# A first MoE pass over 768 tokens in six PSUM banks, later passes of 512, and attention's copies shared out anew

## The chip, the cores and the metric

One Trainium2 chip, of which the kernel uses one core. The metric is the device time of one execution in microseconds. The engines are named as the profile names them: PE (matmuls) with PEld (its weight loads), DVE (VectorE), ACT (ScalarE), POOL (GpSimd) and SP, whose queue issues every DMA here. PSUM, which the matmuls write, has eight banks; one holds 512 float32 per partition.

## The reference

Windowed attention, then two MoE layers that act as plain two-layer networks over 2304 tokens:

```python
scores = q @ k.T / 8 - slope[h] * |i - j|      # batch 4, 8 heads, 576 positions, head size 64
attn = softmax(where(0 <= i - j < 128, scores, -1e9)) @ v
x = attn as [2304 tokens, 512]
h = x @ w1_in;  x = (h * cos(h)) @ w1_out      # w_in 512 x 2048, w_out 2048 x 512
h = x @ w2_in;  g = h if h >= 1 else 0 if h <= -1 else (h + 1)**2 / 4
out = g @ w2_out
```

## The kernel before

**Attention.** 36 pairs, each of 256 tokens and two heads. A pair goes through `do_s` (scores on PE into banks y0 to y3; DVE's fused add-and-minimum, L219; ACT's exp, L226), `normalise` (an add of 1e-9, L232, and a reciprocal, L233, on DVE; the scaling on POOL, L236), `do_t` (transposes into h0 and h1, copied to SBUF by DVE three times in four and by ACT once, `PT`) and `do_v` (banks h2 and h3, copied into `xall` by ACT, `XE`). These stages of successive pairs are interleaved.

**Weights.** They arrive as 64-bit floats in 64 halves, 32 for each layer. `to_f32` turns a half into float32: one ACT pass (L129) into a tile `wu`, of which there are three, then three DVE passes (L130, L132, L134). For layer 1 (`make_w1`) ACT rounds it to a high part (L154) and POOL subtracts for the low part (L78). For layer 2 (`keep_w2`) the float32 half is written to DRAM (`wd`, L165), and is read back and split while layer 1's last chunk runs (`split_w2`).

**MoE.** Tokens go in six chunks of 384 through layer 1, then six through layer 2. A chunk has 16 feature blocks f. `mm_a` makes h of one block with 12 matmuls (4 pieces of the model width, 3 products of high and low parts each) into one of four banks h0 to h3, in turn. `chain` makes g from it: ACT, DVE, ACT, DVE (L320, L321, L325, L326), then a high part by ACT (L337) and a low part by DVE (L78). `mm_b` adds the block into y0 to y3 with 12 more matmuls, three blocks later (`LAG`). `evict` copies y out.

**Order.** PE runs in the order in which the code is written. The other engines run in an order that a scheduler fixed when the program was built; each of them takes its instructions strictly in turn, so one that waits holds all behind it. The scheduler places `to_f32` well ahead of where the code asks for it.

Of the kernel before, what the change touches and what calls it, by code (L numbers as in the profile page):

```python
# [9 lines left out]
F32 = mybir.dt.float32  # L10
# [24 lines left out]
W2LO = "PP"  # L35
GLO = ("D", "D")
# [4 lines left out]
def attention_moe_moe_kernel(  # L41
# [18 lines left out]
    wd = dram.tile([NF, 128, 1024], F32, name="wd")  # L60
    ident = one.tile([128, 128], F32, name="ident")

    xall = one.tile([128, KD, NTOK], F32, name="xall")

    uid = [0]

    def nm(s):
# [90 lines left out]
    w2_kept = [0]  # L158
# [26 lines left out]
    dist8 = []  # L185

    def load(n):
        if n < len(pairs) and "ld" not in pairs[n]:
# [73 lines left out]
    def do_v(p):  # L262
        v_no[0] += 1
        b = ps.tile([128, 512], F32, tag=f"h{2 + v_no[0] % 2}", name=nm("pa"))
        for j in range(2):
            nb = p["w"][j] // 128
            for i in range(nb):
                for h in range(2):
# [5 lines left out]
        x = xall[:, p["hp"], p["b0"] * 128:p["b0"] * 128 + 256]  # L274
        if XE[v_no[0] % len(XE)] == "A":
            ACT.copy(x, b[:, 0:256])
        else:
# [4 lines left out]
    half_pi = one.tile([128, 1], F32, name="half_pi")  # L282

    def split_x(c):
        c["xs"] = [tuple(one.tile([128, T], F32R, tag=f"x{s}{d}", name=nm(f"x{s}")) for s in "hl")
                   for d in range(KD)]
        for d in range(KD):
            hi, lo = c["xs"][d]
            x = xall[:, d, c["t0"]:c["t0"] + T]
            ACT.copy(hi, x)  # L290
            sub_lo(DVE, lo, x, hi)

    h_no = [0]

    def mm_a(c, f):
        hi, lo = weights[c["m"], f]
        h_no[0] = (h_no[0] + 1) % 4
        h = ps.tile([128, 512], F32, tag=f"h{h_no[0]}", name=nm("h"))[:, 0:T]
        n = 0
        for d in range(KD):  # L300
            xh, xl = c["xs"][d]
            s = slice(d * 128, d * 128 + 128)
            for w, x in ((hi, xh), (hi, xl), (lo, xh)):
                PE.matmul(h, lhsT=w[:, 0, s], rhs=x, start=(n == 0), stop=(n == 11))  # L304
                n += 1
                if n == 6:
                    gap()
        chain(c, f, h)
        gap()

    def chain(c, f, h):
        t = small("t")[:, 0:T]
        gh, gl = (small(s, F32R)[:, 0:T] for s in ("gh", "gl"))
        c["g", f] = gh, gl
        if c["m"] == 0:
            k = two.tile([128, T], I32, tag="k", name=nm("k"), bufs=2)

            def s0():

# [22 lines left out]
        later(2, s1)  # L342
        later(3, s2)

    def mm_b(c, f):
# [3 lines left out]
        gh, gl = c["g", f]  # L349
        n = 0  # L350
        for d in range(KD):
            s = slice(d * 128, d * 128 + 128)
            for i, (w, x) in enumerate(((hi, gh), (hi, gl), (lo, gh))):
                PE.matmul(c["y"][d], lhsT=w[:, 1, s], rhs=x,  # L354
                          start=(f == 0 and i == 0), stop=(f == NF - 1 and i == 2))
                n += 1
                if n == 6:
                    gap()
        if f == NF - 1:
            evict(c)  # L360
        if c["m"] == 0 and c["last"]:
            split_w2(f)
        gap()

    def evict(c):
        t0 = c["t0"]
        for d in range(KD):
            s = xall[:, d, t0:t0 + T] if c["m"] == 0 else small("ys")[:, 0:T]
            if d % 2:
                ACT.copy(s, c["y"][d])  # L370
            else:
                DVE.tensor_copy(s, c["y"][d])
            if c["m"]:
                SP.dma_start(out[d * 128:(d + 1) * 128, t0:t0 + T], s)

    chunks = [dict(m=m, t0=i * T, last=i == NCH - 1) for m in range(2) for i in range(NCH)]

    def body():
        load(0)
        dist_sb = two.tile([128, 256], F32, tag="k", name="dist_sb", bufs=2)  # L380
        SP.dma_start(dist_sb, dist)
        load(1)
        DVE.memset(half, 0.5)
        DVE.memset(half_pi, TWO_PI / 4)
        for h in range(NH):

            d8 = one.tile([128, 256], F32, tag=f"x{'hl'[h % 2]}{h // 2}", name=nm("dist8"))
            POOL.tensor_scalar_mul(d8, dist_sb, 2.0 ** (3 - (h + 1)))
            dist8.append(d8)
        make_identity(nc, ident)  # L390
        np_ = len(pairs)
        steps = np_ + AHEAD + 1
        for k in range(-AHEAD, np_ + 1):
            load(k + AHEAD + 1)
            load(k + AHEAD + 2)
            if k + AHEAD < np_:
# [7 lines left out]
            while w1_done[0] * steps < (k + AHEAD) * 2 * PRE:  # L404
                make_w1()
        carried = None
        split_x(chunks[0])
        step = 0
        for ci, c in enumerate(chunks):
            nxt = chunks[ci + 1] if ci + 1 < len(chunks) else None  # L410
            for f in range(NF):
                if c["m"] == 0:
                    if ci == 0:
                        while w1_done[0] < min(2 * (f + W_AHEAD), 2 * NF):
                            make_w1()
# [12 lines left out]
                if f >= LAG:
                    mm_b(c, f - LAG)
            for f in range(NF - LAG, NF - 1):  # L430
                mm_b(c, f)
            carried = c, NF - 1
        mm_b(*carried)
# [58 lines left out]
```

## Time and profile before

| | us |
|---|---|
| runs shown, median of 3 (lowest to highest) | 980.55 (978.40 to 981.01) |
| profiled execution, its own time | 980.5 |
| its span, first to last instruction | 978.7 |
| attention, up to PE's first MoE matmul | 157.6 |
| first two chunks of layer 1, until PE no longer waits | 152.4 |
| the rest, to the last matmul | 665.2 |

Read the stretches apart: a share of the whole span says little here, since attention, the first chunks and the rest have different limits. In a row of a timeline the first number is the start and the second the length; engines overlap the end of one instruction with the start of the next, so the distance of two starts is what an instruction occupies.

### The profile page before, as it was taken

The page shows a single profiled execution, that of the slowest core. Times are in us where ns is not written, and L with a number is a line of the kernel's source. Part 1 is how long each engine was busy: PE and PEld are TensorE (multiplying, and loading weights), DVE is VectorE, ACT ScalarE, POOL GpSimd, SP SyncE. Part 2 cuts the span into 40 slices and gives each one's busy share as a digit, 9 for nine tenths or more (in the row PEclk, how much of TensorE's full clock was granted, in tenths as well). Part 3 has the DMA queues.
Part 4 walks back from the last instruction along what each step waited for, and adds up shares of the span by engine and source line. Part 5 has one row for each costly group of instructions (what it writes and reads, how often), then busy time and mean ns, then how long its engine had stood idle before and what let it go on. Part 6 is the DMA issues. An engine that isn't in the chain of part 4 may idle for free.

```text
span 978.7 us, 14930 instructions
## 1 busy us (share of the span) xinstructions
PE 936.0 (96%) x5712; PEld 894.6 (91%) x5712; DVE 583.7 (60%) x1288; ACT 456.8 (47%) x1024; POOL 176.3 (18%) x150
## 2 busy tenths in 40 slices
PE   5988888998999999999999999999999999999998
PEld 3666667987998999999999999999999999999998
DVE  6899999999898544444345463443444443534433
ACT  5677877655555444344346662332232322323322
POOL 6567665340000000000005660000000000000000
PEclk9998999998999999999999999999999999999999
DMA  6639113447787000000002320000000000000000
GB/s 246 275 121 395 46 45 108 130 151 240 253 283 255 23 2 1 1 1 1 1 1 86 123 71 1 1 33 1 1 33 1 33 1 1 33 1 1 33 1 33
DMA packets 24983, 75.02 MB, mean 77 GB/s; under 512 B 2768, under 2 KB 5968, under 8 KB 24912
## 3 DMA queue, kind: packets, MB, share of 16 engines
q1 hardware_dynamic: 24912, 74.07, 21.9%
q8 instruction: 45, 0.74, 0.3%
q14 instruction: 26, 0.21, 0.1%
HBM read 60.95 MB, written 13.11 MB: 76 GB/s over the span
## 4 chain that ended last, share of the span: by engine, by line
PE 73%; DVE 13%; DMA 5%; issue 4%; ACT 2%; POOL 2%; SPq 0%; POOLq 0%; ACTq 0%; DVEq 0%
PE y L354 35%; PE h L304 34%; DMA wst<-in_w 5%; DVE wu L132 3%; DVE wu L134 3%; DVE sc L219 1%; PE pa L205 1%; PE pa L250 1%; DVE wu L130 1%; POOL sc L236 1%; PE pa L271 1%; DVE pt L256 1%; ACT wu L129 1%; DVE gl L78 1%; ACT sc L226 1%
## 5 line engine op out<-in xcount | busy, mean ns | idle before, releaser
L354 PE MATMUL y<-gl,wh 128*128 128x384 f32 x768 | 259.4, 338 | 4.8 <-DVE gl L78 4.6
L354 PE MATMUL y<-gh,wh 128*128 128x384 f32 x768 | 258.9, 337 | 4.9 <-ACT gh L337 4.9
L354 PE MATMUL y<-gh,wl 128*128 128x384 f32 x768 | 258.2, 336 | 0.0
L304 PE MATMUL h<-xh,wh 128*128 128x384 f32 x768 | 256.8, 334 | 0.0
L304 PE MATMUL h<-xl,wh 128*128 128x384 f32 x768 | 256.7, 334 | 0.0
L304 PE MATMUL h<-xh,wl 128*128 128x384 f32 x768 | 256.6, 334 | 0.0
L78 DVE TENSOR_TENSOR gl<-t,gh 128x384 fp32r<-128x384 f32 x192 | 113.5, 591 | 91.8 <-ACT gh L337 91.5
L331 ACT ACTIVATE t<-t,half 128x384 f32<-128x384 f32 x96 | 59.2, 617 | 206.9 <-DVE t L329 206.9
L354 PEld LDWEIGHTS y<-gl,wh 128*128 128x128 f32 x768 | 145.3, 189 | 7.5 <-DVE gl L78 7.5
L354 PEld LDWEIGHTS y<-gh,wh 128*128 128x128 f32 x768 | 145.1, 189 | 7.4 <-ACT gh L337 7.4
L354 PEld LDWEIGHTS y<-gh,wl 128*128 128x128 f32 x768 | 145.5, 189 | 0.0
L304 PEld LDWEIGHTS h<-xh,wh 128*128 128x128 f32 x768 | 144.5, 188 | 0.2 <-issue 0.2
L337 ACT CAST gh<-t 128x384 fp32r<-128x384 f32 x192 | 98.4, 513 | 98.6 <-DVE t L334 59.8
L304 PEld LDWEIGHTS h<-xh,wl 128*128 128x128 f32 x768 | 144.3, 188 | 0.0
L304 PEld LDWEIGHTS h<-xl,wh 128*128 128x128 f32 x768 | 144.3, 188 | 0.0
L329 DVE TENSOR_SCALAR t<-h 128x384 f32<-128x384 f32 x96 | 53.5, 557 | 112.1 <-PE h L304 112.1
L78 POOL TENSOR_TENSOR wl<-wst,wh 128x512 fp32r<-128x512 f32 x32 | 45.0, 1430 | 315.2 <-ACT wh L175 311.3
L321 DVE SCALAR_TENSOR_TENSOR t<-h,k 128x384 f32<-128x384 f32 x96 | 53.1, 553 | 64.0 <-ACT k L320 64.0
L334 DVE TENSOR_TENSOR t<-h,t 128x384 f32<-128x384 f32 x96 | 53.5, 557 | 55.0 <-ACT t L331 55.0
L226 ACT ACTIVATE sc<-sc,st 128x256 f32<-128x256 f32 (+1 forms) x144 | 69.8, 486 | 32.6 <-DVE st L219 32.3
L236 POOL TENSOR_TENSOR sc<-sc,st 128x512 f32<-128x512 f32 (+1 forms) x72 | 77.7, 1100 | 38.6 <-ACT sc L226 12.7
L325 ACT ACTIVATE t<-t,half_pi 128x384 f32<-128x384 f32 x96 | 59.1, 616 | 45.2 <-DVE t L321 44.9
(42 smaller groups left out, 851.3 us busy)
## 6 DMA issues: line engine op xcount, KB each, us to landing
wst<-in_w SPq DMA_DIRECT2D x64, 512.0 KB, 3.8
qkv<-in_qkv SPq DMA_DIRECT2D x36, 512.0 KB, 9.1
wd<-wu SPq DMA_DIRECT2D x32, 256.0 KB, 2.6
wst<-wd SPq DMA_DIRECT2D x16, 512.0 KB, 3.3
out_t<-ys SPq DMA_DIRECT2D x24, 192.0 KB, 1.9
dist_sb<-in_dist SPq DMA_DIRECT2D x1, 128.0 KB, 3.3
```

Source lines behind the costliest of these rows:

```text
L78: eng.tensor_tensor(out=out, in0=full, in1=f32(hi), op=ALU.subtract)
L132: DVE.scalar_tensor_tensor(out=ui, in0=high, scalar=0x80000000, in1=ui, op0=ALU.bitwise_and, op1=ALU.bitwise_or)
L226: ACT.activation(sc[:, h, 0:w], sc[:, h, 0:w], AF.Exp, bias=st[:, c:c + 1], scale=-1.0, accum_out=st[:, 4 + c:5 + c])
L236: POOL.tensor_tensor(out=sc[:, :, 0:w], in0=sc[:, :, 0:w], in1=st[:, 8 + 2 * j:10 + 2 * j].unsqueeze(2).to_broadcast([128, 2, w]), op=ALU. ...
L304: PE.matmul(h, lhsT=w[:, 0, s], rhs=x, start=(n == 0), stop=(n == 11))
L321: DVE.scalar_tensor_tensor(out=t, in0=h, scalar=INV_2PI, in1=k, op0=ALU.mult, op1=ALU.subtract)
L325: ACT.activation(t, t, AF.Sin, bias=half_pi, scale=TWO_PI)
L329: DVE.tensor_scalar(out=t, in0=h, scalar1=-1.0, scalar2=1.0, op0=ALU.max, op1=ALU.min)
L331: ACT.activation(t, t, AF.Square, bias=half, scale=0.5)
L334: DVE.tensor_tensor(out=t, in0=h, in1=t, op=ALU.max)
L337: ACT.copy(gh, t)
L354: PE.matmul(c["y"][d], lhsT=w[:, 1, s], rhs=x, start=(f == 0 and i == 0), stop=(f == NF - 1 and i == 2))
```

## The change

- Layer 1's first chunk has 768 tokens, as a part of 512 and a part of 256; the other chunks have 512, and layer 2 ends with one of 256. In the first chunk h of the two parts is in h0 and h1, one bank each; y of the first part in y0 to y3, y of the second part in h2 and h3, two pieces to a bank. `mm_b` follows `mm_a` by one block there and by two blocks elsewhere.
- `xall` and the fixed xh and xl tiles give way to a pool of x tiles; `split_x` of the first chunk is written inside the attention loop. `wu` has two tiles instead of three.
- In attention DVE and ACT take the copies after the transposes in turn, and the copies of x in turn. The add of 1e-9 moves from DVE to POOL, the scaling of the distance table from POOL to DVE. `PRE` goes from 6 to 5, and `keep_w2` is spread over 42 of the 48 blocks of the later chunks.

```diff
-T = 384
-NCH = NTOK // T
-LAG = 3
+PARTS = ((((0, 512), (512, 256)), ((768, 512),), ((1280, 512),), ((1792, 512),)),
+         (((0, 512),), ((768, 512),), ((1280, 512),), ((1792, 512),), ((512, 256),)))
+KEEP_STEPS = 42
-PRE = 6
+PRE = 5
-PT = "DDDA"
-XE = "A"
+PT = "DA"
+XE = "DA"
+    chunks = [dict(m=m, parts=parts, last=i == len(PARTS[m]) - 1, lag=1 if len(parts) > 1 else 2)
-        u = two.tile([128, 512], F32, tag="wu", name=nm("wu"), bufs=3)
+        u = two.tile([128, 512], F32, tag="wu", name=nm("wu"), bufs=2)
-        DVE.tensor_scalar_add(st[:, 4:8], st[:, 4:8], 1e-9)
+        POOL.tensor_scalar_add(st[:, 4:8], st[:, 4:8], 1e-9)
-            POOL.tensor_scalar_mul(d8, dist_sb, 2.0 ** (3 - (h + 1)))
+                DVE.tensor_scalar_mul(dist8[h], dist_sb[0], 2.0 ** (3 - (h + 1)))
...
-    def mm_a(c, f):
+    def mm_a(c, i, f):
+        if len(c["parts"]) > 1:
+            tag = f"h{i}"
+        else:
+            h_no[0] = (h_no[0] + 1) % 4
+            tag = f"h{h_no[0]}"
+        w = c["parts"][i][1]
...
-            c["y"] = [ps.tile([128, 512], F32, tag=f"y{d}", name=nm("y"))[:, 0:T] for d in range(KD)]
+            if i:
+                b = [ps.tile([128, 512], F32, tag=f"h{2 + d}", name=nm("y")) for d in range(2)]
+                c["y", i] = [b[d // 2][:, d % 2 * w:d % 2 * w + w] for d in range(KD)]
...
-                mm_a(c, f)
+                for i in ps_:
+                    mm_a(c, i, f)
...
-                if f >= LAG:
-                    mm_b(c, f - LAG)
+                if f >= lag:
+                    for i in ps_:
+                        mm_b(c, i, f - lag)
```

The scheduler's order on DVE in the first MoE chunk, before, about halfway: from the first use of one block's h to that of the next. The `wu` rows are the conversion of weight halves, the rows on t, h and gl the chain.

```order
L321 SCALAR_TENSOR_TENSOR t_2473<-h_2460,k_2476 128x384
L132 SCALAR_TENSOR_TENSOR wu_2563<-wst_2552,wu_2563 128x512
L134 SCALAR_TENSOR_TENSOR wu_2563<-wst_2552,wu_2563 128x512
L326 TENSOR_TENSOR t_2473<-h_2460,t_2473 128x384
L130 TENSOR_SCALAR wu_2609<-wu_2609 128x512
L132 SCALAR_TENSOR_TENSOR wu_2609<-wst_2561,wu_2609 128x512
L78 TENSOR_TENSOR gl_2475<-t_2473,gh_2474 128x384
L321 SCALAR_TENSOR_TENSOR t_2528<-h_2515,k_2531 128x384
```

The same place in the program now, a block of the 768-token chunk (L364 and L369 are the chain's two uses of h, L80 its low part):

```order
L364 SCALAR_TENSOR_TENSOR t_2595<-h_2582,k_2598 128x512
L132 TENSOR_SCALAR wu_3654<-wu_3654 128x512
L134 SCALAR_TENSOR_TENSOR wu_3654<-wst_3609,wu_3654 128x512
L369 TENSOR_TENSOR t_2595<-h_2582,t_2595 128x512
L364 SCALAR_TENSOR_TENSOR t_2616<-h_2601,k_2618 128x256
L136 SCALAR_TENSOR_TENSOR wu_3654<-wst_3609,wu_3654 128x512
L132 TENSOR_SCALAR wu_3732<-wu_3732 128x512
L80 TENSOR_TENSOR gl_2597<-t_2595,gh_2596 128x512
L369 TENSOR_TENSOR t_2616<-h_2601,t_2616 128x256
L134 SCALAR_TENSOR_TENSOR wu_3732<-wst_3652,wu_3732 128x512
L80 TENSOR_TENSOR g_2617<-t_2616,g_2617 128x256
L136 SCALAR_TENSOR_TENSOR wu_3732<-wst_3652,wu_3732 128x512
```

A block now carries two chains and, with the rest of its rows, three converted halves, where it carried one chain and about one and a half halves. In both programs 17 halves stand ahead of the first chain; ahead of the last chain of the first 768 tokens stand 60 before and 59 now.

POOL in the middle of attention, before: two scalings (sc) for each pair, and the low part of a weight half now and then.

```order
L78 TENSOR_TENSOR wl_1489<-wu_1492,wh_1488 128x512
L236 TENSOR_TENSOR sc_1089<-sc_1089,st_1080 128x512
L236 TENSOR_TENSOR sc_1094<-sc_1094,st_1080 128x512
L236 TENSOR_TENSOR sc_1145<-sc_1145,st_1136 128x512
L236 TENSOR_TENSOR sc_1150<-sc_1150,st_1136 128x512
```

POOL now, between two pairs:

```order
L80 TENSOR_TENSOR wl_927<-wu_930,wh_926 128x512
L256 TENSOR_SCALAR st_728<-st_728 128x4
L260 TENSOR_TENSOR sc_737<-sc_737,st_728 128x512
L260 TENSOR_TENSOR sc_742<-sc_742,st_728 128x512
L80 TENSOR_TENSOR wl_927<-wu_1127,wh_926 128x512
```

The small add (L256) now stands in POOL's queue behind the scalings and the low part that come before it, and DVE's reciprocal, on which the next scaling waits, follows it.

## Rows read from the trace of the kernel before

**Rows 1.** Page, part 1: busy us of each engine (share of the span) x instructions.
```profile
PE 936.0 (96%) x5712; PEld 894.6 (91%) x5712; DVE 583.7 (60%) x1288; ACT 456.8 (47%) x1024; POOL 176.3 (18%) x150
```

**Rows 2.** Windows: stretch, its length, PE, PEld, DVE, ACT, POOL busy, clock, DMA.
```profile
0.00:157.60 157.60, 128.15 (x1104) 92.33 (x1104) 138.00 (x498) 112.14 (x377) 103.81 (x100) 0.96 0.47 179
157.60:310.00 152.40, 142.69 (x774) 137.46 (x773) 143.15 (x248) 90.74 (x172) 27.50 (x18) 0.97 0.65 210
310.00:975.20 665.20, 665.15 (x3838) 664.83 (x3836) 302.57 (x544) 253.45 (x475) 44.98 (x32) 1.00 0.06 21
975.20:978.70 3.50, 0.00 (x0) 0.00 (x0) 0.03 (x1) 0.47 (x1) 0.00 (x0) 0.90 0.59 210
```

**Rows 3.** The chain of waits: start, length, what; at full clock and early on.
```profile
168.57 3.51 PE y L354 x11
...
346.99 2.08 PE y L354 x12
```

**Rows 4.** Windows of PE alone around 169 us: busy, granted clock.
```profile
157.60:164.00 6.40, 6.40 (x38) 1.00 0.55 175
164.00:174.00 10.00, 8.13 (x36) 0.83 0.31 99
```

**Rows 5.** Groups by form, 50 to 150 us: busy, mean ns | idle before, releaser.
```profile
L236 POOL TENSOR_TENSOR sc<-sc,st 128x512 f32<-128x512 f32 x49 | 54.4, 1130 | 34.1 <-ACT sc L226 12.7 <-PE pa L205 9.8 <-DVE st L233 4.2
...
L219 DVE CUSTOM_DVE_ANT_0 sc<-pa,dist 128x256 f32<-128x256 f32 x96 | 35.8, 413 | 1.6 <-PE pa L205 1.4
...
L256 DVE COPY pt<-pa 128x512 f32<-128x512 f32 x36 | 23.7, 672 | 0.5 <-PE pa L250 0.4
...
L232 DVE TENSOR_SCALAR st<-st 128x4 f32<-128x4 f32 x26 | 11.5, 443 | 1.6 <-ACT sc L226 1.5
```

**Rows 6.** Tile st, the same stretch: ns min/median/max.
```profile
L232 DVE TENSOR_SCALAR st<-st x26: 151/364/1031, 51.5 to 147.8; 128x4 f32<-128x4 f32 x26
```

**Rows 7.** Groups by form, whole run: smaller tables, copies and POOL's smallest instruction.
```profile
L388 POOL TENSOR_SCALAR dist<-dist_sb 128x256 f32<-128x256 f32 x8 | 6.7, 848 | 3.5 <-DMA dist_sb<-in_dist 3.3
...
L256 DVE COPY pt<-pa 128x256 f32<-128x256 f32 x6 | 2.5, 415 | 1.6 <-PE pa L250 1.6
...
L482 POOL MEMSET const-float32-0.0<- 128x1 f32 x1 | 0.1, 98 | 0.2 <-issue 0.2
```

**Rows 8.** Timeline, first MoE chunk: a conversion step on DVE beside POOL.
```profile
175.56 1.76 POOL L78 TENSOR_TENSOR wl<-wu,wh 128x512 fp32r<-128x512 f32 x1 [7.46 <-ACT wh L154]
...
176.09 1.52 DVE L130 TENSOR_SCALAR wu<-wu 128x512 uint32<-128x512 uint32 x1
177.53 0.55 DVE L326 TENSOR_TENSOR t<-h,t 128x384 f32<-128x384 f32 x1
```

**Rows 9.** Timeline of DVE later, without POOL: one half's three steps and a chain step.
```profile
264.06 0.43 DVE L130 TENSOR_SCALAR wu<-wu 128x512 uint32<-128x512 uint32 x1 [0.67 <-ACT wu L129]
264.52 0.69 DVE L132 SCALAR_TENSOR_TENSOR wu<-wst,wu 128x512 uint32<-128x512 uint32 x1
265.13 0.55 DVE L321 SCALAR_TENSOR_TENSOR t<-h,k 128x384 f32<-128x384 f32 x1
265.60 0.68 DVE L134 SCALAR_TENSOR_TENSOR wu<-wst,wu 128x512 uint32<-128x512 uint32 x1
```

**Rows 10.** Windows of line L134, once for each half converted: layer 1, then layer 2.
```profile
175.20:221.20 46.00, 11.65 (x14) 1.00 0.47 146
222.60:310.00 87.40, 19.05 (x28) 0.96 0.79 259
```

**Rows 11.** Tile wu, whole run: ns min/median/max; the store's landing in us.
```profile
L129 ACT ACTIVATE wu<-wst x64: 644/671/709, 10.6 to 311.8; 128x512 f32<-128x512 f32 x64
...
DMA to landing us min/median/max: 2.0/2.6/3.9
```

More of the change, by code (lines that the diff above doesn't have):

```diff
@@ L61, in attention_moe_moe_kernel @@
     ident = one.tile([128, 128], F32, name="ident")
-    xall = one.tile([128, KD, NTOK], F32, name="xall")
+    chunks = [dict(m=m, parts=parts, last=i == len(PARTS[m]) - 1, lag=1 if len(parts) > 1 else 2)
+              for m in range(2) for i, parts in enumerate(PARTS[m])]
+    all_parts = [p for parts in PARTS[0] for p in parts]
     uid = [0]
@@ L184, in attention_moe_moe_kernel, with new_x, free_x, x_lo @@
     pairs = [dict(b0=b0, hp=hp) for b0 in range(0, NBLK, 2) for hp in range(NH // 2)]
-    dist8 = []
+    x_tiles = {}
+    x_free = {512: list(range(17)), 256: list(range(4))}
+    def new_x(w, dtype=F32):
+        size = w if x_free[w] else 512
+        slot = size, x_free[size].pop(0)
+        return one.tile([128, size], dtype, tag=f"x{size}.{slot[1]}", name=nm("x"))[:, 0:w], slot
+    def free_x(slot):
+        x_free[slot[0]].append(slot[1])
+    dist8 = {}
+    dist_sb = []
+    def x_lo(n):
+        return one.tile([128, 512 if n < 4 else 256], F32R, tag=f"xl{n}", name=nm("xl"))
     def load(n):
@@ L198, in do_s @@
         banks = []
+        for h in (2 * hp, 2 * hp + 1):
+            if h not in dist8:
+                dist8[h] = x_lo(h)[:, 0:256].bitcast(F32)
+                DVE.tensor_scalar_mul(dist8[h], dist_sb[0], 2.0 ** (3 - (h + 1)))
         for j in range(2):
@@ L273, in do_v @@
                               start=(i == 0), stop=(i == nb - 1))
-        x = xall[:, p["hp"], p["b0"] * 128:p["b0"] * 128 + 256]
+        t0 = p["b0"] * 128
+        o, w = max(a for a in all_parts if a[0] <= t0)
+        if (o, p["hp"]) not in x_tiles:
+            x_tiles[o, p["hp"]] = new_x(w)
+        x = x_tiles[o, p["hp"]][0][:, t0 - o:t0 - o + 256]
         if XE[v_no[0] % len(XE)] == "A":
@@ L284, in split_x @@
     def split_x(c):
[L285 to L291, printed above, removed]
+        c["xs"] = []
+        for i, (o, w) in enumerate(c["parts"]):
+            xs = []
+            for d in range(KD):
+                x, slot = x_tiles.pop((o, d))
+                hi, hi_slot = new_x(w, F32R)
+                lo = x_lo(4 * i + d)[:, 0:w]
+                ACT.copy(hi, x)
+                sub_lo(DVE, lo, x, hi)
+                free_x(slot)
+                xs.append((hi, lo, hi_slot))
+            c["xs"].append(xs)
     h_no = [0]
-    def mm_a(c, f):
+    def mm_a(c, i, f):
         hi, lo = weights[c["m"], f]
-        h_no[0] = (h_no[0] + 1) % 4
-        h = ps.tile([128, 512], F32, tag=f"h{h_no[0]}", name=nm("h"))[:, 0:T]
+        if len(c["parts"]) > 1:
[4 more added lines that the diff above has]
+        w = c["parts"][i][1]
+        h = ps.tile([128, 512], F32, tag=tag, name=nm("h"))[:, 0:w]
         n = 0
         for d in range(KD):
-            xh, xl = c["xs"][d]
+            xh, xl, _ = c["xs"][i][d]
             s = slice(d * 128, d * 128 + 128)
-            for w, x in ((hi, xh), (hi, xl), (lo, xh)):
-                PE.matmul(h, lhsT=w[:, 0, s], rhs=x, start=(n == 0), stop=(n == 11))
+            for a, x in ((hi, xh), (hi, xl), (lo, xh)):
+                PE.matmul(h, lhsT=a[:, 0, s], rhs=x, start=(n == 0), stop=(n == 11))
                 n += 1
@@ L307, in mm_a, with chain @@
                     gap()
-        chain(c, f, h)
+        chain(c, i, f, h)
         gap()
[L311 to L314, printed above, removed]
+    def chain(c, i, f, h):
+        w = c["parts"][i][1]
+        t = small("t")[:, 0:w]
+        if i:
+            g = small("g", F32R)
+            gh, gl = g[:, 0:w], g[:, w:2 * w]
+        else:
+            gh, gl = (small(s, F32R)[:, 0:w] for s in ("gh", "gl"))
+        c["g", i, f] = gh, gl
         if c["m"] == 0:
-            k = two.tile([128, T], I32, tag="k", name=nm("k"), bufs=2)
+            k = two.tile([128, 512], I32, tag="k", name=nm("k"), bufs=2)[:, 0:w]
             def s0():
@@ L343, in chain, with mm_b @@
         later(3, s2)
-    def mm_b(c, f):
+    def mm_b(c, i, f):
         if f == 0:
-            c["y"] = [ps.tile([128, 512], F32, tag=f"y{d}", name=nm("y"))[:, 0:T] for d in range(KD)]
+            w = c["parts"][i][1]
+            if i:
+                b = [ps.tile([128, 512], F32, tag=f"h{2 + d}", name=nm("y")) for d in range(2)]
+                c["y", i] = [b[d // 2][:, d % 2 * w:d % 2 * w + w] for d in range(KD)]
+            else:
+                c["y", i] = [ps.tile([128, 512], F32, tag=f"y{d}", name=nm("y"))[:, 0:w]
+                             for d in range(KD)]
         hi, lo = weights[c["m"], f]
-        gh, gl = c["g", f]
+        gh, gl = c["g", i, f]
         n = 0
@@ L352, in mm_b @@
             s = slice(d * 128, d * 128 + 128)
-            for i, (w, x) in enumerate(((hi, gh), (hi, gl), (lo, gh))):
-                PE.matmul(c["y"][d], lhsT=w[:, 1, s], rhs=x,
-                          start=(f == 0 and i == 0), stop=(f == NF - 1 and i == 2))
+            for k, (a, x) in enumerate(((hi, gh), (hi, gl), (lo, gh))):
+                PE.matmul(c["y", i][d], lhsT=a[:, 1, s], rhs=x,
+                          start=(f == 0 and k == 0 and not (i and d % 2)),
+                          stop=(f == NF - 1 and k == 2 and (i == 0 or d % 2 == 1)))
                 n += 1
@@ L363, in mm_b, with evict @@
         gap()
-    def evict(c):
-        t0 = c["t0"]
+    def evict(c, i):
+        o, w = c["parts"][i]
         for d in range(KD):
-            s = xall[:, d, t0:t0 + T] if c["m"] == 0 else small("ys")[:, 0:T]
+            if c["m"] == 0:
+                x_tiles[o, d] = new_x(w)
+                s = x_tiles[o, d][0]
+            else:
+                s = small("ys")[:, 0:w]
             if d % 2:
-                ACT.copy(s, c["y"][d])
+                ACT.copy(s, c["y", i][d])
             else:
-                DVE.tensor_copy(s, c["y"][d])
+                DVE.tensor_copy(s, c["y", i][d])
             if c["m"]:
-                SP.dma_start(out[d * 128:(d + 1) * 128, t0:t0 + T], s)
-    chunks = [dict(m=m, t0=i * T, last=i == NCH - 1) for m in range(2) for i in range(NCH)]
+                SP.dma_start(out[d * 128:(d + 1) * 128, o:o + w], s)
     def body():
         load(0)
-        dist_sb = two.tile([128, 256], F32, tag="k", name="dist_sb", bufs=2)
-        SP.dma_start(dist_sb, dist)
+        dist_sb.append(two.tile([128, 256], F32, tag="k", name="dist_sb", bufs=2))
+        SP.dma_start(dist_sb[0], dist)
         load(1)
@@ L384, in body @@
         DVE.memset(half_pi, TWO_PI / 4)
-        for h in range(NH):
-            d8 = one.tile([128, 256], F32, tag=f"x{'hl'[h % 2]}{h // 2}", name=nm("dist8"))
-            POOL.tensor_scalar_mul(d8, dist_sb, 2.0 ** (3 - (h + 1)))
-            dist8.append(d8)
         make_identity(nc, ident)
@@ L397, in body @@
                 do_s(pairs[k + AHEAD])
+            elif k + AHEAD == np_:
+                split_x(chunks[0])
             if 0 <= k + AHEAD - 1 < np_:
@@ L406, in body @@
         carried = None
-        split_x(chunks[0])
         step = 0
@@ L410, in body @@
             nxt = chunks[ci + 1] if ci + 1 < len(chunks) else None
+            lag, ps_ = c["lag"], range(len(c["parts"]))
             for f in range(NF):
@@ L415, in body @@
                             make_w1()
-                    elif not c["last"]:
+                    else:
                         step += 1
-                        while w2_kept[0] * (NF * (NCH - 2)) < step * 2 * NF:
+                        while w2_kept[0] < 2 * NF and w2_kept[0] * KEEP_STEPS < step * 2 * NF:
                             keep_w2()
-                    elif f == 0:
+                    if c["last"] and f == 0:
                         for i in range(2):
                             stage_f32(i)
-                mm_a(c, f)
+                for i in ps_:
+                    mm_a(c, i, f)
                 if f == 0 and carried is not None:
-                    mm_b(*carried)
-                if f == NF - 1 and nxt is not None:
-                    split_x(nxt)
-                if f >= LAG:
-                    mm_b(c, f - LAG)
[L430 to L433, printed above, removed]
+                    for i in range(len(carried["parts"])):
+                        mm_b(carried, i, NF - 1)
+                if f == NF - 1:
+                    for xs in c["xs"]:
+                        for x in xs:
+                            free_x(x[2])
+                    if nxt is not None:
+                        split_x(nxt)
+                if f >= lag:
+                    for i in ps_:
+                        mm_b(c, i, f - lag)
+            for f in range(NF - lag, NF - 1):
+                for i in ps_:
+                    mm_b(c, i, f)
+            carried = c
+        mm_b(carried, 0, NF - 1)
         run_due(True)
```

2 lines of the change are left out of this document (1 added, 1 removed).

## The prediction

> **What bounds the kernel now.** I read the busy shares first, then the windows by stage, then the chain of waits, then groups, tiles and timelines inside the two stages that are not dense. PE is busy 96% of the span [rows 1], but the windows divide it: attention takes 157.6 us, in which DVE is busy 138.0, ACT 112.1, POOL 103.8; two chunks take 152.4 us, in which PE is busy 142.7 and DVE 143.2; the remaining 665.2 us have no PE idle time to speak of; 3.5 us of eviction and output follow [rows 2].
>
> In the dense part 12 matmuls of 384 columns take 2.08 us, so one takes 173.3 ns [rows 3]. At 2.4 GHz 384 columns alone are 160.0 ns, so 13.3 ns are something else. At half clock 11 matmuls take 3.51 us, 319 ns each [rows 3], and the columns alone at 1.2 GHz are 320: there the extra is hidden. PE fell to that clock after it had waited near 167 us [rows 4].
>
> The two chunks hold 768 matmuls, 768 x 173.3 = 133.1 us. They take 152.4, so 19.3 us are lost: PE waits for DVE, which besides the chains converts the weight halves. A layer 1 half comes every 46.0 / 14 = 3.29 us, a layer 2 half every 87.4 / 28 = 3.12 us [rows 10]. Without POOL beside it a half occupies DVE for 0.46 + 0.61 + about 0.60 = 1.67 us and a 384-column chain step 0.47 us, by distances of starts [rows 9]. With POOL's subtraction beside it a step of 0.43 us lasted 1.52 [rows 8, 9]: DVE and POOL hold each other up.
>
> **Part 1, wider matmuls.** Per layer there were six chunks of 384 columns and there are now four passes of 512 and one of 256. That is 384 matmuls per pass and layer: before 2 x 6 x 384 = 4608, now 3072 of 512 and 768 of 256, 768 fewer with the same columns. If the 13.3 ns belong to the instruction, a 512 takes 213.3 + 13.3 = 226.7 ns and a 256 takes 106.7 + 13.3 = 120.0: 696.3 + 92.2 = 788.5 us against 4608 x 173.3 = 798.7. Gain 10.2 us. The trace has one width of this matmul only, so both ends count: if the extra goes with the columns, the gain is 0; if a longer matmul hid it altogether, the columns alone would be 737.3 and the gain 61. I take 10.2, since half clock shows the columns at their bare price, so that the extra looks like a cost of each weight load or start. All of it is on the path, because PE is dense there.
>
> **Part 2, attention.** DVE is the busiest engine, so its sum counts.
> - Transposed copies: DVE had 54 of 72, now 36. It sheds 16 of 512 columns, each 0.60 us as it occupies DVE (a 512-column step of [rows 9], against 0.67 in length [rows 5]), and two of 256 at 0.34: 10.3 us. It gains 18 copies of x, 256 columns from PSUM, nearest row 0.415 in length [rows 7], 0.34 as occupied: 6.1 us. Net -4.2. The 18 copies lie on ACT instead, which sheds 18 of x; ACT has 45 us idle in the stage [rows 2].
> - The add: 36 on DVE at 443 ns mean [rows 5], 16 us in length, but only 151 ns when nothing holds it [rows 6], 5.4 us. The rest is waiting for POOL's scalings. On POOL the add costs between 0.1 and 0.85 us [rows 7]; I take 0.2, as it has four columns. POOL can carry 7 us more. But there it stands behind the scalings and the low part of a weight, and DVE's reciprocal, with the next pair's instructions behind it, waits for it. So the wait does not go, it is moved to the reciprocal in part. I count half, -7 us; the ends are -16 and +6, the latter if each of 36 pairs waits 0.36 us longer than I count (a third of a scaling [rows 5]).
> - The table: 8 scalings go from POOL (6.7 us before POOL's first normalisation [rows 7]) to DVE; both ends of this are in the start-up, where qkv loads set the pace: 0.
> - `split_x` of 768 tokens is 4 x 0.60 + 4 x 0.34 = 3.7 us of DVE, instead of 4 x 0.47 = 1.9: +1.9. `PRE` moves nothing: both orders have 17 halves ahead of the first chain.
>
> Sum -9.3; I take -8 (-18 to +6), since ACT's and POOL's latencies fill part of a shortened cycle.
>
> **Part 3, the first pass.** Dense it is 16 x 24 x (226.7 + 120.0) = 133.1 us, as long as the two chunks before, and 42 halves against 43 stand in it. DVE's own work: a block carries 3 x 0.60 + 3 x 0.34 = 2.8 us of chain, 45 us in 16 blocks, where 32 chains of 1.4 us were 45 too. So DVE has the same to do beside the same matmuls. What differs: three halves per block make 5.0 + 2.8 = 7.8 us of DVE against 8.3 of PE for layer 2's halves, a fit, and about 10 us for layer 1's, which POOL stretches. `wu` has two tiles: one is held for 0.67 (ACT) + about 2.6 (three steps and the chain steps between) + 2.6 (store) us [rows 11], and 0.3 of hand-over, 6.2 us; two make one half each 3.1 us, which is today's 3.12, with nothing to spare. h has one bank per part: `mm_a` of the next block must wait for the chain's second use of h, while PE has 5.6 us of other matmuls. Sum: 3.3 us to the first chain, 15 x 3.3 for layer 1's halves, 27 x 3.1 for layer 2's, 9.8 of PE work behind the last chain, 2 at the change to the next chunk: 148 to 153. I take +2 against 152.4 (bounds -19.3, all waits gone, and +27, below).
>
> **Part 4, the ends.** The four last halves are now converted while layer 2's weights are split, with PE at 5.4 us a block: +1. The last chunk is 256 wide, its eviction a third shorter (3.5 us with output [rows 2]): -0.3.
>
> Sum: 980.5 - 10.2 - 8 + 2 + 1 - 0.3 = 965.0 us, made against the profiled execution's 980.5 us, of which 1.8 lie outside its span; the median of the runs shown is 980.55, the same.
>
> **Rivals.**
> - The extra of a matmul goes with its columns (or is as large for the work as before): the matmul gain is 0, 975 us. For it: only one width is in the trace. Against: half clock. The Trainium skill, TensorE: Matmul & The Clock Gate, "Back-to-back issue gap", gives a warm spacing of columns / 2.4 plus 2.5 ns. By that rule, an estimate, 768 fewer matmuls save 1.9 us and the sum would be 973; but it gives 162.5 ns for 384 columns, where this trace has 173.3 [rows 3].
> - The first pass becomes slower. Mechanism: with one bank for h and a lag of one block DVE can no longer run late while PE goes on. If ACT waits in turn for `wu`'s store (up to 3.9 us [rows 11]), k and the sine wait behind it, DVE waits behind the chain, PE behind DVE. Layer 2's halves at 4.1 us instead of 3.1 add 27 us: 992 us. It decides from about 3.8 us a half. For it: the ring has nothing to spare. Against: stores land in 2.6 as a rule, and DVE's own sum leaves half a us per block.
> - The first pass fits entirely: 8.3 us of PE per block cover DVE's 7.8, and layer 1's halves ahead of need cost little: the 19.3 us nearly go, 948 us. Against: POOL's subtractions still stretch 15 halves by 0.7 us or more each.
> - Attention gains nothing, since the reciprocal waits for POOL: 973 us.
>
> **How the numbers follow.** Forecast 0.50 (its own range 957 to 975); column rival 0.13; slow first pass 0.14; fitting first pass 0.13; no gain in attention 0.10. A measurement of this kernel tells 0.3% from no change, 977.6 to 983.5 us. The forecast and the fitting pass are faster (0.63); of the column rival and of attention without gain, which lie just under the bound, a little over half (0.12). The slow pass gives 0.12 of slower, with 0.02 from the others; 0.11 is left for the same. The range 948 to 983 leaves out most of the slow pass and a little under the fitting one.
>
> **What would show it.** Spacing of the 512-column matmuls in the dense part: 2.72 us for 12 in the chain of waits is right, 2.77 is the column rival, under 2.65 more gain than forecast. PE's first MoE matmul at about 149.5 us; at 157 or later attention gained nothing, and the idle time before reciprocals on DVE says why. From there to the end of PE's waits about 150 us; more, with ACT's conversion pass waiting for a store, is the slow pass; 135 or less the fitting one. The forecast is wrong if the first pass costs 15 us more than now, or if the extra per matmul was no fixed cost and attention gave nothing either.

## The result, and the profile after

The changed kernel is a little slower: 987.09 us, median of 7 runs, against 980.95 of the kernel before beside it, ratio 1.0051 [1.0028, 1.0073]; in a second series 984.56 us (983.18 to 986.05), ratio 1.0046 [1.0031, 1.0062]. Two of the 7 ran at a lower granted clock, 1051 and 1302 us at 0.844 and 0.657 on average, which the ratio leaves out, and the median of the other five is 985.38 us. Forecast were 965.0 us, range 948 to 983. The rows below are of an execution of 983.18 us, span 981.4, in the second series.

Windows by stage of the changed kernel (columns as in [rows 2]):

```profile
0.00:160.90 160.90, 130.40 (x1105) 93.16 (x1105) 132.64 (x474) 117.53 (x382) 109.24 (x129) 0.97 0.48 178
160.90:320.00 159.10, 145.63 (x790) 125.91 (x789) 141.39 (x242) 90.82 (x171) 25.01 (x17) 0.96 0.60 196
320.00:500.00 180.00, 180.00 (x796) 149.10 (x795) 75.81 (x112) 71.70 (x113) 0.00 (x0) 1.00 0.00 1
500.00:560.00 60.00, 56.02 (x237) 45.08 (x236) 32.14 (x43) 30.38 (x54) 30.78 (x20) 0.97 0.41 132
560.00:977.80 417.80, 417.80 (x2025) 353.73 (x2023) 181.29 (x284) 129.03 (x213) 17.50 (x12) 1.00 0.05 16
977.80:981.40 3.60, 0.07 (x1) 0.00 (x0) 0.17 (x1) 0.37 (x1) 0.00 (x0) 0.88 0.44 146
```

Compare line by line with [rows 2]. Attention is 160.9 us long instead of 157.6, although DVE does 5.4 us less in it (132.6 for 138.0). The stretch from 320 us on is dense, except for one place, 500 to 560 us, that was dense before. The matmuls themselves became as much cheaper as forecast. The chain of waits shows one block of 512 columns and, in the last pass, one of 256:

```profile
326.71 2.72 PE h L342 x12
...
929.06 1.43 PE h L342 x12
```

2.72 / 12 is 226.7 ns, 1.43 / 12 is 119.2; the median distance of starts is 227 and 120 ns. So all MoE matmuls back to back are 788.5 us, where they were 798.7 [rows 3].

From these a budget. From PE's first MoE matmul to the end of its last are 977.8 - 160.9 = 816.9 us, of which 816.9 - 788.5 = 28.4 are lost; before it was 975.2 - 157.6 - 798.7 = 18.9. Of the 28.4, 6.4 lie between 520 and 540 us (distances of starts beyond 227 ns, added up), so 22.0 in the first pass and a little behind it. Matmuls -10.2, attention +3.3, first pass 22.0 - 18.9 = +3.1, the place at 520 us +6.4: +2.6, and the spans differ by 981.4 - 978.7 = 2.7.

**Attention.** The waits of DVE and of ACT in the first 160.9 us (us in total, times, longest):

```profile
DVE st L257 <- POOL st L256: 19.5, 16, 3.6
```
```profile
ACT sc L250 <- DVE st L243: 23.8, 24, 3.4
ACT wu L131 <- POOL wl L80: 7.7, 6, 2.7
```

The first line is the add, now on POOL (L256): DVE's reciprocal (L257) waits 19.5 us for it. In the second the exps wait for DVE, for which they waited 32.3 us before. The last has grown from 0.7 us: with two tiles of `wu`, ACT's conversion pass waits for the tile in which POOL still reads. How the two meet is seen in a timeline (start, length, engine, and in brackets the idle time ahead and what ended it):

```profile
105.02 1.26 POOL L80 TENSOR_TENSOR wl<-wu,wh 128x512 fp32r<-128x512 f32 x1
...
106.32 0.66 ACT L131 ACTIVATE wu<-wst 128x512 f32<-128x512 f32 x1 [1.84 <-POOL wl L80]
...
106.89 0.49 ACT L250 ACTIVATE sc<-sc,st 128x256 f32<-128x256 f32 x1
...
108.12 0.22 POOL L256 TENSOR_SCALAR st<-st 128x4 f32<-128x4 f32 x1 [1.84 <-ACT sc L250]
...
108.38 0.18 DVE L257 RECIPROCAL st<-st 128x4 f32<-128x4 f32 x1 [1.66 <-POOL st L256]
```

ACT stands 1.84 us at a conversion of a weight half that no engine needs before the MoE stage; the exps (L250) stand behind it in ACT's queue; so the add, the reciprocal and the scaling come late here.

**520 to 540 us.** The last chunk of layer 1, the timeline at the loss:

```profile
530.42 0.66 ACT L131 ACTIVATE wu<-wst 128x512 f32<-128x512 f32 x1 [3.22 <-DMA wst<-in_w]
...
530.98 1.12 ACT L177 CAST wh<-wst 128x512 fp32r<-128x512 f32 x2
...
531.66 3.40 POOL L80 TENSOR_TENSOR wl<-wst,wh 128x512 fp32r<-128x512 f32 x2 [4.67 <-ACT wh L177]
532.01 0.61 ACT L380 CAST gh<-t 128x512 fp32r<-128x512 f32 x1
532.30 1.65 DVE L136 SCALAR_TENSOR_TENSOR wu<-wst,wu 128x512 uint32<-128x512 uint32 x1
...
532.68 0.49 PE L404 MATMUL y<-gh,wh 128*128 128x512 f32 x1 [1.25 <-ACT gh L380]
533.87 1.75 DVE L80 TENSOR_TENSOR gl<-t,gh 128x512 fp32r<-128x512 f32 x1
...
535.67 0.50 PE L404 MATMUL y<-gl,wh 128*128 128x512 f32 x1 [2.50 <-DVE gl L80]
...
537.50 0.63 PE L404 MATMUL y<-gl,wh 128*128 128x512 f32 x1
537.92 0.63 PE L404 MATMUL y<-gh,wl 128*128 128x512 f32 x1
```

One of the four last halves waits 3.22 us for its load, at the head of ACT's queue. Behind it stand the splits of layer 2's weights and gh, for which PE waits 1.25 us; then DVE's conversion and gl run beside POOL's subtractions and last 1.65 and 1.75 us, PE waits 2.50 more. After the two waits seven starts lie 427 ns apart (537.50 and 537.92 are two of them), granted clock 0.78 on average from 536.4 to 544 us: for these matmuls 2.4 GHz fell to 1.2. DVE and POOL holding each other up is described by the Trainium skill, SBUF — State Buffer, "Terms" (an exclusive lock on a shared port pair, held for the whole instruction); the 1.65 us here, against 0.68 for the same conversion step without POOL [rows 9], and the 1.75 us of gl, against 0.69 on average from 320 to 500 us, where POOL is idle, agree with it.

**First pass.** PE's largest wait is at the second block:

```profile
165.05 0.28 PE L342 MATMUL h<-x,wl 128*128 128x256 f32 x1
171.03 0.79 PE L342 MATMUL h<-x,wh 128*128 128x512 f32 x1 [5.70 <-DVE t L369]
```

It needs the bank h0, which the first block's chain has not yet read for the last time, and there is no earlier block whose `mm_b` could fill the time. Nearly all of PE's waits up to 320 us are of this kind, 13.2 us; before they were for g, 9.5 us. ACT in turn waits for the store of `wu`, as it did not before:

```profile
ACT wu L131 <- DMA wd<-wu: 22.2, 21, 2.5
```

### The profile page after: what moved, and what is told of

Its sections match the earlier page's. It is cut to its first block, busy times and chain, and to the rows that moved or that the text cites. A ratio compares the mean times of both kernels' runs of the same rounds, so it can differ in the third digit from the quotient of the medians.

```text
span 1049.2 us, 13072 instructions
## 1 busy us (share of the span) xinstructions
PE 1010.4 (96%) x4944; PEld 786.5 (75%) x4944; DVE 566.5 (54%) x1152; ACT 441.6 (42%) x932; POOL 182.1 (17%) x178
## 3 DMA queue, kind: packets, MB, share of 16 engines
q1 hardware_dynamic: 24336, 74.07, 20.4%
## 4 chain that ended last, share of the span: by engine, by line
PE 82%; DVE 7%; POOL 5%; ACT 3%; issue 2%; DMA 1%; SPq 0%; POOLq 0%; ACTq 0%
PE h L342 39%; PE y L404 39%; POOL sc L260 3%; POOL wl L80 2%; DVE sc L243 2%; DVE wu L134 1%; PE pa L229 1%; PE pa L274 1%; PE pa L295 1%; ACT sc L250 1%; DVE wu L136 1%; DVE wu L132 1%; ACT wu L131 1%; DMA qkv<-in_qkv 0%; DVE pt L280 0%
## 5 line engine op out<-in xcount | busy, mean ns | idle before, releaser
L342 PE MATMUL h<-x,wh 128*128 128x512 f32 (+1 forms) x640 | 253.1, 396 | 10.3 <-DVE t L369 10.2
L342 PE MATMUL h<-x,wl 128*128 128x512 f32 (+1 forms) x640 | 253.2, 396 | 0.0
L342 PE MATMUL h<-xl,wh 128*128 128x512 f32 (+1 forms) x640 | 252.9, 395 | 0.0
L404 PE MATMUL y<-gh,wl 128*128 128x512 f32 (+1 forms) x576 | 232.6, 404 | 0.0
L404 PE MATMUL y<-gl,wh 128*128 128x512 f32 (+1 forms) x576 | 232.4, 403 | 0.2 <-DVE gl L80 0.2
L404 PE MATMUL y<-gh,wh 128*128 128x512 f32 (+1 forms) x576 | 231.5, 402 | 0.0
L342 PEld LDWEIGHTS h<-x,wh 128*128 128x128 f32 x640 | 125.0, 195 | 42.0 <-DVE t L369 11.2
L342 PEld LDWEIGHTS h<-x,wl 128*128 128x128 f32 x640 | 125.3, 196 | 29.6
L80 DVE TENSOR_TENSOR gl<-t,gh 128x512 fp32r<-128x512 f32 (+1 forms) x144 | 101.8, 707 | 82.5 <-ACT gh L380 81.3
L380 ACT CAST gh<-t 128x512 fp32r<-128x512 f32 (+1 forms) x144 | 85.8, 595 | 74.8 <-DVE t L377 52.1
L80 POOL TENSOR_TENSOR wl<-wst,wh 128x512 fp32r<-128x512 f32 x32 | 47.8, 1515 | 346.4 <-ACT wh L177 342.5
L364 DVE SCALAR_TENSOR_TENSOR t<-h,k 128x512 f32<-128x512 f32 x80 | 50.6, 634 | 94.0 <-ACT k L363 93.6
L250 ACT ACTIVATE sc<-sc,st 128x256 f32<-128x256 f32 (+1 forms) x144 | 69.9, 487 | 24.5 <-DVE st L243 23.9
```

The source lines that it names most:

```text
L80: eng.tensor_tensor(out=out, in0=full, in1=f32(hi), op=ALU.subtract)
L342: PE.matmul(h, lhsT=a[:, 0, s], rhs=x, start=(n == 0), stop=(n == 11))
L364: DVE.scalar_tensor_tensor(out=t, in0=h, scalar=INV_2PI, in1=k, op0=ALU.mult, op1=ALU.subtract)
L380: ACT.copy(gh, t)
L404: PE.matmul(c["y", i][d], lhsT=a[:, 1, s], rhs=x, start=(f == 0 and k == 0 and not (i and d % 2)), stop=(f == NF - 1 and k == 2 and (i == ...
```

## The experiments

**e1_after**, the changed kernel again, for a profile.

> The changed kernel once more, unchanged, for a profile at full clock. If the extra 13.3 ns of a matmul are a fixed cost, 12 matmuls of 512 columns take 2.72 us in the dense part and PE needs 788 us for the MoE matmuls; if they go with the columns, 2.77 us and 799 us. The time itself is 984 to 988 us by either, so with the fixed cost 20 us must be found in attention and the first pass, with the column cost 5 us.

984.56 us, ratio 1.0046 [1.0031, 1.0062]; its rows are those above.

**e2_att_old** and **e3_add_dve**, the changed kernel with attention's moves undone, all or the add alone:

```diff
-PT = "DA"            # e2
-XE = "DA"
+PT = "DDDA"
+XE = "A"
-        POOL.tensor_scalar_add(st[:, 4:8], st[:, 4:8], 1e-9)      # e2, e3
+        DVE.tensor_scalar_add(st[:, 4:8], st[:, 4:8], 1e-9)
```

> The changed kernel with attention as before: three copies in four on DVE after the transposes, x copied by ACT, the add on DVE. If moving these is what attention lost by, PE's first MoE matmul comes 4 us or more earlier than in the changed kernel and the time falls by as much; if they helped and something else is slow, it rises by about 8 us.

> The changed kernel with only the small add of 1e-9 back on DVE. If DVE's reciprocal waits for POOL's queue (the theory), attention is 5 to 10 us shorter than in the changed kernel, shorter than before as well, and the time falls by that. If the add on POOL is harmless, the time is the same or up to 5 us longer.

986.6 us, 1.0063 [1.0038, 1.0089], and 985.69, 1.0054 [1.0033, 1.0076]; first MoE matmul at 161.9 and 162.0 us. e2 fits neither of its outcomes, e3 the second, the add on POOL harmless. With two tiles of `wu`, undoing the moves brings nothing back that can be told from the changed kernel's 1.0046. The first matmul by itself compares attention only roughly, since the scheduler places the conversions anew with each edit: ahead of it ACT starts 17 halves in the changed kernel, 16 in e3 and 14 in e2.

**e4_split**, the first pass cut in two, with four h banks and a lag of two blocks:

```diff
-PARTS = ((((0, 512), (512, 256)), ((768, 512),), ((1280, 512),), ((1792, 512),)),
+PARTS = ((((0, 512),), ((512, 256),), ((768, 512),), ((1280, 512),), ((1792, 512),)),
```

> The changed kernel with the first pass of 768 tokens cut into a pass of 512 and one of 256, in four banks for h with a lag of two blocks, as its other passes. If one bank for h is what makes PE wait, the first 768 tokens lose less, and the time falls by 5 to 10 us. If DVE's conversions set that stage, PE loses more in the 512 pass, since it has less to do per block, and the time is the same or longer by up to 15 us.

980.73 us, 1.0010 [0.9998, 1.0021], about 3.8 us less than the changed kernel. Its profile shows no loss at 520 to 540 us (more chunks, and so all halves early), and 25.6 us lost ahead of 340 us, where the changed kernel lost 22.0. The gain is thus the last conversions', which this edit was not meant to touch; e8 takes them by themselves.

**e5_before_wu2**, the kernel before with the smaller ring alone:

```diff
-        u = two.tile([128, 512], F32, tag="wu", name=nm("wu"), bufs=3)
+        u = two.tile([128, 512], F32, tag="wu", name=nm("wu"), bufs=2)
```

> The kernel before with one edit: the ring wu of converted weight halves has two tiles instead of three, as the changed kernel has it. Theory A (the ring of two is what the changed kernel loses in attention: ACT's conversion pass L129 waits for POOL's low part of the half before last, and the exps queued behind it on ACT come late): PE's first MoE matmul moves from 157.6 us to 160 or later, the waits of ACT L129 for POOL grow from under 1 us to several us, and the time rises by 3 to 6 us, 983 to 986 us. Rival B (the ring has no part in it; the loss comes from split_x among the last pairs or from the copies): first MoE matmul at 157.6 +- 0.7 and 980.2 +- 1 us.

984.74 us, 1.0045 [1.0026, 1.0064]: theory A. Window of attention, and from the tile view of `wu`, for the whole run, the idle time ahead of its instructions (us, times):

```profile
0.00:160.90 160.90, 131.35 (x1105) 94.20 (x1105) 139.30 (x500) 111.71 (x377) 105.02 (x100) 0.97 0.46 175
```
```profile
  POOL wl L78: 27.5, 20
  DMA wd<-wu: 23.9, 19
```

Before, the first was 0.7 us and the second did not occur. In part they take the place of ACT's waits for the loads of the halves, 27.8 us before and 0.5 here. PE's first MoE matmul is at 160.9 us, as in the changed kernel. This profile is of the longest of nine executions, so how the loss divides between attention and the first chunks is less sure than its sum.

**e6_attention_moves** and **e12_copies_alone**, the kernel before with the moves alone:

```diff
-PT = "DDDA"          # e6, e12
-XE = "A"
+PT = "DA"
+XE = "DA"
-        DVE.tensor_scalar_add(st[:, 4:8], st[:, 4:8], 1e-9)       # e6
+        POOL.tensor_scalar_add(st[:, 4:8], st[:, 4:8], 1e-9)
```

> The kernel before with the three moves of attention alone: transposed copies alternate between DVE and ACT, x copies alternate too, the add of 1e-9 goes from DVE to POOL. All else (chunks of 384, wu of three tiles, split_x behind the loop, table on POOL) stays. The prediction's Part 2 counted -4.2 and -7 for these: first MoE matmul near 147 to 150 us, time 969 to 973. Theory A (the moves gain little, since DVE's wait is only handed from the add to the reciprocal, and the rest is lost by the ring): first matmul 155 to 157, time 977 to 980. Rival B (the moves themselves cost, since ACT's exps wait behind copies): first matmul at 159 or later, time 982 to 985.

> The kernel before with the copies alone divided between DVE and ACT; the add stays on DVE. The prediction gave them -4.2 us. Theory A (DVE is not short of its own time but waits for the other engines in a loop ACT - DVE - POOL, so relief of one engine gives little): first MoE matmul 156 to 158, 979 to 980.5 us. Rival B (DVE's sum sets attention): first matmul at 153 to 154, 976 us.

e6: 979.98 us, 0.9985 [0.9973, 0.9996], the upper end of theory A, with the first matmul at 157.7 us, where it was 157.6. Groups of DVE up to there, of before and of e6 (count, busy, mean ns, idle ahead):

```profile
L256 DVE COPY pt<-pa 128x512 f32<-128x512 f32 x48 | 31.6, 675 | 1.2 <-PE pa L250 1.1
L232 DVE TENSOR_SCALAR st<-st 128x4 f32<-128x4 f32 x36 | 14.7, 408 | 4.1 <-ACT sc L226 4.1
L134 DVE SCALAR_TENSOR_TENSOR wu<-wst,wu 128x512 uint32<-128x512 uint32 x15 | 13.8, 922 | 0.0
L233 DVE RECIPROCAL st<-st 128x4 f32<-128x4 f32 x36 | 6.0, 168 | 0.2
```
```profile
L256 DVE COPY pt<-pa 128x512 f32<-128x512 f32 x32 | 21.5, 673 | 0.0
L134 DVE SCALAR_TENSOR_TENSOR wu<-wst,wu 128x512 uint32<-128x512 uint32 x17 | 18.0, 1061 | 0.0
L278 DVE COPY xall<-pa 128x256 f32<-128x256 f32 x17 | 7.0, 412 | 0.0
L233 DVE RECIPROCAL st<-st 128x4 f32<-128x4 f32 x36 | 6.2, 173 | 13.6 <-POOL st L232 13.2
```

The add's 14.7 us have left DVE, but the reciprocal now waits 13.2, and a conversion step became 139 ns longer beside a busier POOL (119.1 us of work for 103.8). The copies are 4.0 us less (31.6 to 21.5, 2.5 to 1.6 for the narrow ones, and 7.0 of x added). e12: 983.16 us, 1.0030 [1.0019, 1.0042], first matmul at 160.2 us. The copies alone cost 2.5 us, against both theories; POOL's waits for the reciprocal grew to 22.2 us from 7.0. The traces show where freed time went: ahead of the first chain 19 halves are converted in e6 and e12, against 17 in the kernel before and in the changed kernel. Two halves are about 5 us of DVE (0.675 + 0.922 + 0.922 us for the three steps of one, means of attention before), more than the copies freed. Some of it comes back later: PE's losses by distances of starts in the first chunks are 18.6 us before, 17.1 in e12 and 15.8 in e6. That the two halves are what made e12 slower is not shown.

**e7_split_behind**, the changed kernel with `split_x` behind attention's loop:

```diff
-            elif k + AHEAD == np_:
-                split_x(chunks[0])
...
         carried = None
+        split_x(chunks[0])
```

> The changed kernel with one edit: split_x of the first pass is issued behind the loop over pairs, as in the kernel before, not ahead of the last normalise. Rival B (the subtractions of split_x, 1.2 to 1.4 us each on DVE in the last four pairs, are what attention loses): PE's first MoE matmul from 160.9 to 158 or 159 us and 982 us. Theory A (the ring): first matmul stays at 160.9 or becomes later, as the splits then stand in front of it, 984 to 987 us.

988.08 us, 1.0063 [1.0047, 1.0079]; first matmul at 161.4 us, and the wait at the second block 7.0 us. Where the split stands is not the cause; its new place is, if anything, the better one.

**e8_conv_early**, the changed kernel with the last halves earlier:

```diff
-KEEP_STEPS = 42
+KEEP_STEPS = 32
```

> The changed kernel with KEEP_STEPS 32 instead of 42: all 32 halves of layer 2 are issued ahead of the last 512 chunk of layer 1, so that the loads of layer 2's float32 weights no longer take tiles of ring ld ahead of the last four halves. Theory A (the 6.4 us that PE loses at 520 to 540 us are those four halves, converted beside layer 2's splits): the loss there goes, the halves lie at 300 to 330 us, where PE has none to wait for; 978 to 979 us. Rival B (the four halves only lose the same time at 300 to 330 us, where DVE is the bound): the loss of 3 to 6 us turns up there and the time stays at 983 to 985 us.

980.16 us, 0.9991 [0.9978, 1.0004], 5 us less than the changed kernel: theory A, though 1 us above its figure. The stretch is dense:

```profile
500.00:560.00 60.00, 60.00 (x267) 49.70 (x266) 25.34 (x35) 34.04 (x57) 31.03 (x21) 1.00 0.27 88
```

First matmul here at 163.7 us, with the same instructions in attention as at 160.9 above: single executions differ by that much, so the verdicts on attention rest on the timed ratios.

**e9_ring3_conv**, **e10_ring3_split**, **e11_add_dve_ring3**: `KEEP_STEPS` 32 and three tiles of `wu` in all; e10 also cuts the first pass as e4, e11 also puts the add back as e3.

```diff
-        return two.tile(list(shape), dtype, tag="s", name=nm(name), bufs=12)
+        return two.tile(list(shape), dtype, tag="s", name=nm(name), bufs=11)
-        u = two.tile([128, 512], F32, tag="wu", name=nm("wu"), bufs=2)
+        u = two.tile([128, 512], F32, tag="wu", name=nm("wu"), bufs=3)
-KEEP_STEPS = 42
+KEEP_STEPS = 32
```

> The changed kernel with the ring wu of three tiles again (for its 2 KB the ring s has 11 tiles instead of 12) and KEEP_STEPS 32. Theory A (the ring cost 3.3 us in attention and about 1 behind it, the last conversions 4 to 6): first MoE matmul at 157 to 158 us, 975.5 to 977 us, 0.4 to 0.5% faster than before. Rival B (in the changed kernel something else holds attention, since DVE's reciprocal waits for POOL's add, and the ring adds nothing to that): first matmul at 160 to 164 as in the runs with two tiles, 980 us.

> As the run with the ring of three and KEEP_STEPS 32, and the first pass in two, one of 512 columns and one of 256, each with four h banks and a lag of two blocks. Theory A (the wait of PE at 165 us, 4.6 to 7.1 us long, comes of one h bank per part): that wait goes, but layer 1's halves come at the same pace and so are awaited in the 512 pass instead; 974 to 977 us, within 1 us of the run before it. Rival B (the wide first pass is itself what loses): 970 to 973 us.

> As the run with the ring of three and KEEP_STEPS 32, and the add of 1e-9 on DVE again. Theory A (the add on POOL is worth about nothing: DVE's wait for it is as long as the add was): within 1.5 us of that run, 975 to 978. Rival B (with the ring of three, DVE's waits for POOL's add are what sets attention): first matmul 3 to 5 us earlier, 972 us.

e9: 978.16 us, 0.9971 [0.9960, 0.9982], first matmul at 159.6. e10: 975.43, 0.9942 [0.9930, 0.9954]. e11: 973.84, 0.9936 [0.9923, 0.9949], first matmul at 157.2. e9 lies between its theories, 976 and 980 us, and so does its first matmul. That the ring is what ACT waited for in attention is shown: its conversion pass waits 7.7 us for POOL's low part there in the changed kernel, 6.9 in e8 and not at all in e9. DVE's reciprocal still waits 18.0 us for POOL's add in e9. With three tiles the split is worth 2.7 us; with two it brought nothing that can be told (e4 against e8, 1.0010 and 0.9991). Its mechanism is seen in PE's waits from 158 to 320 us, of e9 and of e10:

```profile
PE h L342 <- DVE t L369: 14.2, 10, 5.5
```
```profile
PE y L404 <- DVE gl L80: 5.9, 11, 1.5
PE y L404 <- ACT gh L380: 5.9, 5, 2.3
```

With four h banks PE no longer waits for a bank but for g, 2.4 us less in all. The add on DVE is worth 3 to 4 us (e11 against e9), nearer to rival B of e11 than to its theory A, though the same edit brought nothing with two tiles (e3).

**e13_all_four** (split, ring, `KEEP_STEPS` and add together), **e14_copies_back** (e11 with the copies of before), **e15_s11** (e8 with the ring s of 11 tiles):

> The changed kernel with the four edits together: ring wu of three tiles (ring s 11), KEEP_STEPS 32, the first pass in two, the add of 1e-9 on DVE. If the gains add up (2.7 us of the split, 4.4 of the add, both measured against the run with ring and KEEP_STEPS alone): 971 us, 1% under before. Rival: the split and the add remove the same waits, 973 to 974.

> As the run with the ring of three, KEEP_STEPS 32 and the add on DVE (973.8 us), but with the copies as in the kernel before: three of four transposed copies on DVE, all of x on ACT. Theory A (the copies alone cost 2.5 us in the kernel before, so they cost here too): 971 to 972 us. Rival B (the prediction's -4.2 for the copies, as DVE's sum): 977 to 978 us.

> The changed kernel with KEEP_STEPS 32 and the ring s of 11 tiles, but wu still of two. It prices the smaller s, which the runs with wu of three also carry. Theory A (s is not short): 980.2 +- 1 us, as with 12 tiles, so that the third tile of wu alone is worth 2 us. Rival B (the smaller s costs 1 to 2 us): 981.5 to 983 us, and the third tile of wu is worth as much more.

e13: 971.66 us, 0.9909 [0.9891, 0.9928], 0.9% under the kernel before and the fastest of all: the gains add up to within 1 us, as expected. PE's first MoE matmul is at 157.3 us, and PE loses 20.4 us behind it; before it was 157.6 and 18.9. So with the four edits the rest of the change costs and brings about nothing, and what is left is the 10.2 us of the wider matmuls less the 1.5 us that PE loses more. Its first stretches:

```profile
0.00:156.80 156.80, 126.46 (x1096) 91.14 (x1098) 139.72 (x507) 116.92 (x380) 99.13 (x93) 0.96 0.48 183
156.80:316.00 159.20, 148.31 (x803) 124.85 (x800) 147.93 (x256) 94.81 (x177) 24.24 (x17) 0.98 0.66 215
```

e14: 975.20 us, 0.9944 [0.9927, 0.9961], not told apart from e11, and neither theory: here the copies neither cost nor bring. e15: 981.73 us, 1.0012 [0.9999, 1.0026], the rival: against e8 the ring s of 11 tiles costs about 2 us. e9, with the third tile of `wu`, is 0.41% under e15, 4 us: the ring costs as much in the changed kernel as in the kernel before (e5).

## Why the prediction was wrong

- **Part 1, wider matmuls, -10.2: right.** 226.7 and 120.0 ns were forecast, 227 and 120 measured, and the column rival (2.77 us for 12) is out. By the warm spacing of isolated matmuls in the Trainium skill, TensorE: Matmul & The Clock Gate, "Back-to-back issue gap", 512 columns would be, an estimate, 215.8 ns and 12 of them 2.59 us; the trace has 2.72, so the measurement decides against it here.
- **Part 2, attention, -8: this step failed**, with +3.3 in its place: 11.3 of the 18.2 us between the forecast of 965.0 and the profiled 983.18. "I count half, -7 us" for the add: e6 shows that the wait moved from the add to the reciprocal whole. The rival "attention gains nothing, since the reciprocal waits for POOL" named this, at 0.10. The -4.0 for the copies is there as DVE's work (34.1 to 30.1 us of copies in e6), but not as time: in e6 and e12 two more halves were converted in its place, and in the changed kernel e2 brings nothing back. And `wu` with two tiles was priced for the first pass alone; in attention, where 15 halves are converted, it was given no price. e5 against the kernel before and e9 against e15 show 4 us for it in all; how much of that is attention's, single profiles do not tell.
- **Part 3, first pass, +2: right in size,** +3.1 by the budget, but in part by luck. The wait for the one h bank is what PE lost by (5.70 us at the second block, where the "5.6 us of other matmuls" do not exist). ACT's waits for `wu`'s store, with which its 3.1 us a half were worked out, are there too, but no run shows that they cost time in this stage: with three tiles PE loses 23.1 us there (e9), with two 22.0 (e8) and 29.8 (e15). The rival of 992 us, which builds on the latter, is out: a 22 us loss in place of the 46 that it needs.
- **Part 4, last conversions, +1: mis-sized,** 6.4 us. It counted DVE's work beside a dense PE. What it left out is the order on ACT: the halves' loads come behind those of layer 2's weights, and gh and the splits stand behind the pass that waits for them. e8 removes 5 us by moving the four halves. The -0.3 for a shorter eviction did not come: the last stretch is 3.6 us, 3.5 before.

The two failed parts, 11.3 and 5.4 us, are 16.7 of the 18.2 us between 965.0 and the profiled 983.18; the first pass has 1.1 and the end 0.4. The median of that series lies 1.4 us above the profiled execution.

**Open.** The add on POOL lowers the time by 0.45%, 4 us, in the kernel before with divided copies (ratios of e12 and e6), makes no difference that can be told in the changed kernel (e3), and costs 3 to 4 us there once `wu` has three tiles (e11 to e9). All three engines are in that loop, and the scheduler orders their work anew with each edit; which of the two decides was not separated. `PRE` and the scaling of the table had no run of their own.

## What to carry to other kernels

A smaller ring must be priced in every stage that uses it, and its price is not the work that waits but what stands behind that work in its engine's queue. In a loop over three engines, taking work off the busiest one need not shorten it: ask who starts earlier, and see whether the idle time merely changes its line, or the scheduler fills the freed time with other work. Work moved to the end of a stage should be checked against the loads that are in front of it there.

## What the runs showed of the hardware

At full clock a matmul of this kind costs its columns plus 13.3 ns at 256, 384 and 512 columns alike; at half clock the 512 take 427 ns, which is the columns alone. After two waits of PE at 531 to 536 us, 1.25 and 2.50 us long, seven matmuls ran at half clock, which with the one on either side of them cost 1.6 us. The add of four columns takes 220 ns on POOL (median; 548 at most) and 263 on DVE (151 at least, 1051 at most); beside that DVE's reciprocal waited 13.2 us (e6) and 19.5 us (changed kernel) in all for the add on POOL.
